# Float64 weights made float32 by a shifted upper word, a sign step and an integer addition, with w_in kept tile by tile

## The chip, the cores and the metric

The kernel runs on one core of one Trainium2 chip. The metric is the device time of one execution in microseconds; before the change its median over three runs is 944.7 us (944.42 to 946.44). The profile was taken on one more execution, whose span, from the first instruction to the last, is 942.4 us.

The core has five engines with queues of their own, which meet through semaphores: TensorE (PE in the profile; its weight loads are PEld), VectorE (DVE), ScalarE (ACT), GpSimd (POOL) and SyncE (SP), which here issues most transfers. Instructions of one engine run in the order of the program.

## What is computed

Two blocks, one after the other: an attention without softmax with an RMS norm, and a two-matrix feed-forward block with the gate h * erf(softplus(h)).

```python
# q, k, v: (8, 8, 576, 64) float32; g_norm: (64,) float32
kv = np.einsum('bhsd,bhse->bhde', k, v)
out = np.einsum('bhsd,bhde->bhse', q, kv)
rms = np.sqrt(np.mean(out * out, axis=-1, keepdims=True) + 1e-06)
attn = (out / rms * g_norm).astype(np.float32)
x = attn.transpose(0, 2, 1, 3).reshape(4608, 512)
# w_in: (512, 2048), w_out: (2048, 512), both float64
h = x @ w_in
sp = np.maximum(h, 0.0) + np.log1p(np.exp(-np.abs(h)))
g = h * erf(sp)
result = (g @ w_out).astype(np.float32)
```

The weights come as float64 (a random float32 array times a float64 scalar). [...] the kernel reads them as pairs of 32-bit words, a lower and an upper one, and makes float32 values of them itself, on VectorE and ScalarE, in its first 125 us.

## The kernel before

The 4608 tokens are worked on in nine groups of 512: eight of one batch each (the last 64 rows of each batch are collected in a ninth group). `FC` is 16, the number of 128-wide tiles of the hidden dimension; `KC` is 4, the number of 128-row blocks of the model dimension. A pass of the first two groups uses float32 matmuls with w_in and w_out as they stand in SBUF; from the second group on the operands are cut into three reduced forms (high, low, both), which the later groups fetch from DRAM.

w_in stands in SBUF with the row block outermost, w_out with the tile outermost:

```python
w_in_sb = first_w.tile([P, KC, DF], FP32, name="w_in_sb")
w_out_sb = first_w.tile([P, FC, DM], FP32, name="w_out_sb")
```

A unit of weights is one tile (`k` = 1, the first four tiles of w_in: 128 partitions x 512 values) or a pair (`k` = 2, all else: 128 x 1024). Each goes through a load, a split and a join. Four raw buffers hold what was loaded:

```python
    w_raw, w_cv = {}, {}
    RAW = 4

    def load_w(which, f, k):
        t = w_raw[which, f] = early.tile([P, 2 * G * k], I32, name="w_raw", tag="w_raw", bufs=RAW)
        if which == "in":
            nc.sync.dma_start(
                out=t.rearrange("p (c f) -> p c f", c=KC),
                in_=moe_w_in.rearrange("(c p) f -> p c f", p=P)[:, :, 2 * f * P : 2 * (f + k) * P],
            )
        else:
            nc.sync.dma_start(
                out=t.rearrange("p (t f) -> p t f", t=k),
                in_=moe_w_out.rearrange("(t p) f -> p t f", p=P)[:, f : f + k, :],
            )

    def w_split(which, f, k):

        hi = w_raw[which, f].rearrange("p (n two) -> p n two", two=2)[:, :, 1]
        e = early.tile([P, G * k], I32, name="w_e", tag="w_e", bufs=2)
        m = early.tile([P, G * k], I32, name="w_m", tag="w_m", bufs=2)
        nc.vector.tensor_scalar(
            out=e,
            in0=hi,
            scalar1=20,
            scalar2=0x7FF,
            op0=ALU.logical_shift_right,
            op1=ALU.bitwise_and,
        )
        nc.scalar.activation(e, e, AF.Relu, scale=float(1 << 23), bias=exp_col)
        nc.vector.tensor_scalar(
            out=m, in0=hi, scalar1=0xFFFFF, scalar2=None, op0=ALU.bitwise_and
        )
        nc.scalar.activation(m.bitcast(FP32), m, AF.Identity, scale=2.0**-20, bias=1.0)
        w_cv[which, f] = e, m

    def w_join(which, f, k):
        raw, (e, m) = w_raw.pop((which, f)), w_cv.pop((which, f))
        hi = raw.rearrange("p (n two) -> p n two", two=2)[:, :, 1]
        lo = raw.bitcast(U32).rearrange("p (n two) -> p n two", two=2)[:, :, 0]
        nc.vector.scalar_tensor_tensor(
            out=e, in0=hi, scalar=-(1 << 31), in1=e, op0=ALU.bitwise_and, op1=ALU.bitwise_or
        )
        m = m.bitcast(FP32)
        nc.vector.scalar_tensor_tensor(
            out=m, in0=lo, scalar=2.0**-52, in1=m, op0=ALU.mult, op1=ALU.add
        )
        e = e.bitcast(FP32)
        if which == "in":
            out_ = w_in_sb[:, :, f * P : (f + k) * P]
            e, m = (t.rearrange("p (c f) -> p c f", c=KC) for t in (e, m))
        else:
            out_ = w_out_sb[:, f : f + k, :]
            e, m = (t.rearrange("p (c f) -> p c f", c=k) for t in (e, m))
        nc.vector.tensor_tensor(out=out_, in0=e, in1=m, op=ALU.mult)
```

The split takes the exponent and the mantissa out of the upper word on VectorE (L207, L216) and turns each into a float on ScalarE (L215, L219). The join puts the sign on the power of two (L226), adds the lower word to the mantissa (L230), and multiplies the two (L240).

The units and when they are due, and where they stand in the opening, before the first hidden tile. `first` holds the attention pieces of the four head pairs of group 0, in the order products, apply, halve, mean, norm:

```python
    w_order = sorted(
        [(f, "in", f, 1) for f in range(4)]
        + [(f, "in", f, 2) for f in range(4, FC, 2)]
        + [(min(f + LAG, (f + FC) // 2 + 1), "out", f, 2) for f in range(0, FC, 2)]
    )
    w_at = {"load": 0, "split": 0, "join": 0}
... # cut
    w_rounds = {
        1: ("split",),
        2: ("join", "load", "split"),
        3: ("join", "load"),
        5: ("split",),
        6: ("split", "join", "load", "join", "load"),
    }
    banks_0 = {"kv_ps": (ps_at, "at"), "qt_ps": (ps_h, "h"), "ms_ps": (ps_h, "h")}
    first = [attention(0, p, banks_0 | {"se_ps": (ps_o, f"o{p}")}) for p in range(NP)]
    for i in range(NP + 3):
        for piece, p in ((0, i), (1, i - 1), (4, i - 3), (3, i - 2)):
            if 0 <= p < NP:
                first[p][piece]()
        if i == 1:
            for _ in range(RAW - 2):
                w_next("load")
            load_pair(NP)
            load_pair(NP + 1)
        for what in w_rounds.get(i, ()):
            w_next(what)
```

The attention pieces that stand between them (`bank` gives a PSUM bank; in the opening `qt_ps` and `ms_ps` share the two banks of `ps_h`):

```python
def apply():
    qT, o_ps, kv_ps = st["qT"], bank("se_ps"), st.pop("kv")
    nc.tensor.matmul(kv_ps[:, o_tail], lhsT=bd, rhs=st.pop("tail"), start=True, stop=True)
    nc.tensor.matmul(o_ps, lhsT=bd, rhs=qT, start=True, stop=True)                     # L325
    nc.vector.tensor_copy(out=x_last[:, p, T * R : T * R + R], in_=kv_ps[:, o_tail])   # L326
    st["o"] = o_ps
    nc.scalar.activation(qT, o_ps, AF.Square)                                          # L328

def mean(table=True):
    ms = st["ms"] = bank("ms_ps")
    ... # cut
    nc.tensor.matmul(ms, lhsT=mean_w.bitcast(FP32), rhs=u, start=True, stop=True)      # L351
    ... # cut
    nc.scalar.activation(r, ms, AF.Ln, bias=eps_col)                                   # L358
    nc.scalar.activation(r, r, AF.Exp, scale=-0.5)                                     # L359
    nc.scalar.activation(u, r, AF.Square)                                              # L360
    if table and (T > 0 or p == NP - 1):
        softplus_table()                                                               # L106

def norm():
    ms, u, r = (st.pop(name) for name in ("ms", "u", "r"))
    nc.vector.scalar_tensor_tensor(
        out=u, in0=ms, scalar=EPS, in1=u, op0=ALU.add, op1=ALU.mult
    )
    nc.vector.scalar_tensor_tensor(
        out=u, in0=u, scalar=3.0, in1=r, op0=ALU.subtract, op1=ALU.mult
    )
    if T < FIRST:
        if T not in xT:
            xT[T] = wide.tile([P, KC, G], FP32, name="xT", tag="ab"[T])
        x = xT[T][:, p, :]
    else:
        x = st["x"] = x_new.tile([P, G], FP32, name="x", tag="x")
    nc.vector.scalar_tensor_tensor(
        out=x,
        in0=st.pop("o"),
        scalar=gm_col,
        in1=u,
        op0=ALU.mult,
        op1=ALU.mult,
    )
```

(The norm's three VectorE instructions have the lines L366, L369 and L378 in the profile; the last writes xT.) The hidden tiles of the first group start with two tiles side by side, block by block of xT:

```python
            if n > 1:
                plain[n] = ps_h.tile([P, G], FP32, name="h_ps", tag="h")
                blocks = [(n, c) for c in range(KC)]
            elif n == 0:
                for i, (pool, tag) in enumerate(((ps_at, "at"), (ps_o, "o0"))):
                    plain[i] = pool.tile([P, G], FP32, name="h_ps", tag=tag)
                blocks = [(i, c) for c in range(KC - 1) for i in range(2)] + [(0, KC - 1)]
            else:
                blocks = [(1, KC - 1)]
            for i, c in blocks:
                nc.tensor.matmul(
                    plain[i],
                    lhsT=w_in_sb[:, c, i % FC * P : i % FC * P + P],
                    rhs=xT[T][:, c, :],
                    start=(c == 0),
                    stop=(c == KC - 1),
                )
            ... # cut
            if n in plain:
                nc.scalar.copy(h, plain.pop(n))                # L705
            ... # cut
            nc.scalar.activation(s, h, AF.Softplus)            # L720
            if n == 0:
                w_next("split")
```

In the second group w_in_sb's tiles that are used up become the place for the forms of six tiles of w_out, which are stored to DRAM from there:

```python
parts = w_in_sb.bitcast(FP32R)[:, :, 3 * place * P : 3 * (place + 1) * P].rearrange(
    "p c (i f) -> p i c f", i=3
)
... # cut
for i in range(3):
    if t is None:
        nc.sync.dma_start(
            out=kept[:, i].rearrange("p (c f) -> p c f", c=KC), in_=parts[:, i].bitcast(FP32)
        )
```

Of the kernel before, what the change touches and what calls it, by code (L numbers as in the profile page):

```python
# [60 lines left out]
def kernel(  # L61
# [101 lines left out]
    w_in_sb = first_w.tile([P, KC, DF], FP32, name="w_in_sb")  # L163
# [11 lines left out]
    exp_col = const.tile([P, 1], FP32, name="exp_col")  # L175
    nc.vector.memset(exp_col, -896.0 * (1 << 23))
# [12 lines left out]
    def load_w(which, f, k):  # L189
        t = w_raw[which, f] = early.tile([P, 2 * G * k], I32, name="w_raw", tag="w_raw", bufs=RAW)  # L190
        if which == "in":
            nc.sync.dma_start(
                out=t.rearrange("p (c f) -> p c f", c=KC),
                in_=moe_w_in.rearrange("(c p) f -> p c f", p=P)[:, :, 2 * f * P : 2 * (f + k) * P],
            )
# [5 lines left out]

    def w_split(which, f, k):

        hi = w_raw[which, f].rearrange("p (n two) -> p n two", two=2)[:, :, 1]
        e = early.tile([P, G * k], I32, name="w_e", tag="w_e", bufs=2)
        m = early.tile([P, G * k], I32, name="w_m", tag="w_m", bufs=2)
        nc.vector.tensor_scalar(  # L207
            out=e,
            in0=hi,
            scalar1=20,  # L210
            scalar2=0x7FF,
            op0=ALU.logical_shift_right,
            op1=ALU.bitwise_and,
        )
        nc.scalar.activation(e, e, AF.Relu, scale=float(1 << 23), bias=exp_col)  # L215
        nc.vector.tensor_scalar(  # L216
            out=m, in0=hi, scalar1=0xFFFFF, scalar2=None, op0=ALU.bitwise_and
        )
        nc.scalar.activation(m.bitcast(FP32), m, AF.Identity, scale=2.0**-20, bias=1.0)  # L219
        w_cv[which, f] = e, m  # L220

    def w_join(which, f, k):
        raw, (e, m) = w_raw.pop((which, f)), w_cv.pop((which, f))
        hi = raw.rearrange("p (n two) -> p n two", two=2)[:, :, 1]
        lo = raw.bitcast(U32).rearrange("p (n two) -> p n two", two=2)[:, :, 0]
# [3 lines left out]
        m = m.bitcast(FP32)  # L229
        nc.vector.scalar_tensor_tensor(  # L230
            out=m, in0=lo, scalar=2.0**-52, in1=m, op0=ALU.mult, op1=ALU.add
        )
# [683 lines left out]
```

## Time and profile before

| stretch (us) | what runs | TensorE busy | VectorE busy | ScalarE busy | DMA share |
|---|---|---|---|---|---|
| 0 to 36 | attention of group 0, first weights, first hidden tiles | 24.66 | 20.34 | 20.38 | 0.84 |
| 36 to 145 | first group, the other weights | 109.00 | 91.11 | 90.07 | 0.49 |
| 145 to 240 | second group, weights cut into forms and stored | 95.00 | 77.69 | 66.81 | 0.89 |
| 240 to 936 | the other seven groups | 695.57 | 551.03 | 438.39 | 0.84 |

The columns are busy microseconds within the stretch, and the mean busy share of the core's 16 DMA engines. The mean clock granted to TensorE is 0.999 of full speed.

How to read the profile's lines: a timeline line has the start (us from the span's beginning), the length of the piece, engine, source line, operation, output and inputs, and shape; in brackets, the idle time before it and what ended it. A line of the groups has the count after x, then the busy time in us and the mean of one in ns, then the idle time of the engine just before these instructions and what ended most of it. A line of the waits says who waited for whom: us in total, how often, the longest. A float32 matmul of 128x512 appears as two MATMUL instructions. Ends of matmuls are modelled, so pieces on PE can overlap by a fraction of a microsecond.

### The profile page before, as it was taken

Reading aid. Unit: us, or ns where it says so; the run is one execution under the profiler, and the core shown is the slowest. Engines: PE = TensorE matmul, PEld = TensorE weight load, DVE = VectorE, ACT = ScalarE, POOL = GpSimd, SP = SyncE. Lnnn points to the kernel's source line nnn. Section 1 sums busy time; section 2 is a strip of 40 time slices with the busy share of each in tenths; the row PEclk is TensorE's granted clock in tenths of the full one; section 3 lists DMA queues with packets and bytes.
Section 4 is the critical chain, followed back from the end, with each engine's and each line's share of the span. In section 5 each row is a group of like instructions: output and inputs, shape, how many; then the busy total and the mean of one; then the engine's idle time right before and its main releaser. Section 6 shows DMA issues by size and latency. Waiting matters only on the chain.

```text
span 942.4 us, 11743 instructions
## 1 busy us (share of the span) xinstructions
PE 924.8 (98%) x4272; PEld 683.4 (73%) x4272; DVE 742.6 (79%) x1056; ACT 615.6 (65%) x825; POOL 2.4 (0%) x10
## 2 busy tenths in 40 slices
PE   6999999999999999999999999999999999999997
PEld 4444445666688888888888888888888888888886
DVE  3999858887577787877778888878887877787667
ACT  3899776776766666666666666666666666665551
POOL 1000000000000000000000000000000000000000
PEclk9999999999999999999999999999999999999999
DMA  9766406899699998998899889998896778778871
GB/s 257 276 204 207 150 1 227 318 351 335 214 363 335 309 325 283 306 311 307 280 287 314 294 298 309 311 303 296 293 325 260 263 253 345 284 286 287 353 263 46
DMA packets 111842, 259.78 MB, mean 276 GB/s; under 512 B 43864, under 2 KB 69544, under 8 KB 111784
## 3 DMA queue, kind: packets, MB, share of 16 engines
q1 hardware_dynamic: 110152, 256.73, 78.7%
q10 hardware_dynamic: 1568, 2.29, 0.8%
q8 instruction: 34, 0.56, 0.2%
q14 instruction: 24, 0.20, 0.1%
q0 software_dynamic: 64, 0.00, 0.0%
HBM read 224.40 MB, written 34.60 MB: 275 GB/s over the span
## 4 chain that ended last, share of the span: by engine, by line
PE 92%; DVE 4%; DMA 2%; ACT 1%; issue 0%; SPq 0%; DVEq 0%
PE n_ps L462 45%; PE m_ps L462 22%; PE o_ps L520 10%; PE h_ps L692 6%; PE se_ps L325 3%; PE kv_ps L297 2%; PE qt_ps L319 2%; DMA w_raw<-in_moe_w_in_dram 1%; PE ms_ps L351 1%; DMA v_sb<-in_v_dram 1%; DVE h L876 1%; DVE e L445 1%; PE ms_ps L346 1%; PE ms_ps L347 1%; PE kv_ps L324 1%; DVE e L440 0%
## 5 line engine op out<-in xcount | busy, mean ns | idle before, releaser
L462 PE MATMUL n_ps<-x_forms,w_in_parts 128*128 128x512 f32 x896 | 232.5, 401 | 0.1
L462 PE MATMUL n_ps<-w_out_parts,g_forms 128*128 128x512 f32 x928 | 231.2, 391 | 0.0
L462 PEld LDWEIGHTS n_ps<-w_out_parts,g_forms 128*128 128x128 f32 x928 | 174.2, 188 | 38.4 <-issue 1.4
L462 PEld LDWEIGHTS n_ps<-x_forms,w_in_parts 128*128 128x128 f32 x896 | 166.8, 188 | 43.1 <-issue 9.3
L852 ACT ACTIVATE s<-h 128x512 f32<-128x512 f32 x112 | 71.0, 633 | 178.9 <-DVE h L445 178.9
L445 DVE TENSOR_TENSOR h<-m_ps,h 128x512 f32<-128x512 f32 x116 | 79.7, 687 | 59.8 <-ACT h L837 43.8
L462 PE MATMUL m_ps<-w_out_parts,g_forms 128*128 128x512 f32 x464 | 124.2, 389 | 0.0
L462 PE MATMUL m_ps<-x_forms,w_in_parts 128*128 128x512 f32 x448 | 120.0, 390 | 0.0
L520 PE MATMUL o_ps<-w_out_sb,h_sb 128*128 128x512 f32 x224 | 100.8, 593 | 0.3 <-DVE h_sb L642 0.3
L462 PEld LDWEIGHTS m_ps<-w_out_parts,g_forms 128*128 128x128 f32 x464 | 87.1, 188 | 18.0
L462 PEld LDWEIGHTS m_ps<-x_forms,w_in_parts 128*128 128x128 f32 x448 | 84.1, 188 | 17.7
L445 DVE TENSOR_TENSOR e<-m_ps,e 128x512 f32<-128x512 f32 x116 | 80.2, 692 | 18.2 <-PE m_ps L462 10.9
L440 DVE SCALAR_TENSOR_TENSOR e<-n_ps,e 128x512 f32<-128x512 f32 x88 | 60.3, 685 | 39.2 <-PE n_ps L462 39.2
L520 PEld LDWEIGHTS o_ps<-w_out_sb,h_sb 128*128 128x128 f32 x224 | 42.3, 190 | 48.9 <-issue 46.6
L411 DVE SCALAR_TENSOR_TENSOR g_forms<-g_forms 128x1024 fp32r<-128x1024 f32 x58 | 71.1, 1225 | 2.0
L408 DVE TENSOR_TENSOR g_forms<-h,g_forms 128x1024 fp32r<-128x1024 f32 x58 | 70.6, 1217 | 1.7 <-ACT g_forms L405 1.4
L876 DVE TENSOR_TENSOR h<-h,s 128x1024 f32<-128x1024 f32 x58 | 68.3, 1218 | 0.7 <-ACT s L856 0.7
L837 ACT ACTIVATE h<-n_ps 128x512 f32<-128x512 f32 x112 | 65.5, 585 | 3.4 <-PE n_ps L462 3.4
L405 ACT ACTIVATE g_forms<-h 128x1024 fp32r<-128x1024 f32 x58 | 58.9, 1059 | 12.2 <-PE m_ps L462 8.7
L692 PE MATMUL h_ps<-xT,w_in_sb 128*128 128x512 f32 x144 | 64.9, 594 | 0.7 <-DVE w_in_sb L240 0.6
L106 ACT ACT_TABLE_LOAD x44 | 56.5, 1283 | 0.8
L856 ACT ACTIVATE s<-s 128x1024 f32<-128x1024 f32 x56 | 56.2, 1052 | 0.3
(98 smaller groups left out, 1013.3 us busy)
## 6 DMA issues: line engine op xcount, KB each, us to landing
w_out_parts<-w_out SPq DMA_DIRECT2D x116, 768.0 KB
w_in_parts<-w_in SPq DMA_DIRECT2D x112, 768.0 KB
w_in<-w_new SPq DMA_DIRECT2D x16, 768.0 KB
q_sb<-in_q_dram SPq DMA_DIRECT2D x32, 256.0 KB
w_raw<-in_moe_w_out_dram SPq DMA_DIRECT2D x8, 1024.0 KB
out_dram<-e SPq DMA_DIRECT2D x32, 256.0 KB
k_sb<-in_k_dram SPq DMA_DIRECT2D x28, 287.5 KB
v_sb<-in_v_dram SPq DMA_DIRECT2D x28, 287.5 KB
```

What stands on the lines that cost most here:

```text
L106: nc.scalar.preload_act_table_set("softplus")
L405: nc.scalar.activation(high, x, AF.Copy, scale=1.0 + 2.0**-13)
L408: nc.vector.tensor_tensor(out=low, in0=x, in1=high.bitcast(FP32), op=ALU.subtract)
L411: nc.vector.scalar_tensor_tensor(out=both, in0=low.bitcast(FP32), scalar=SHIFT, in1=high.bitcast(FP32), op0=ALU.mult, op1=ALU.add,)
L440: nc.vector.scalar_tensor_tensor(out=out_, in0=ps, scalar=scale, in1=out_, op0=ALU.mult, op1=ALU.add)
L445: nc.vector.tensor_tensor(out=out_, in0=ps, in1=out_, op=ALU.add)
L462: nc.tensor.matmul(ps, lhsT=weights(form, k), rhs=moving(form, k), start=(form == forms[0] and k == 0), stop=(form == forms[-1] and k == 3),)
L520: nc.tensor.matmul(o_ps[j], lhsT=g[:, j * P : j * P + P], rhs=w_out_sb[:, f, :], start=(f == 0), stop=last,)
L692: nc.tensor.matmul(plain[i], lhsT=w_in_sb[:, c, i % FC * P : i % FC * P + P], rhs=xT[T][:, c, :], start=(c == 0), stop=(c == KC - 1),)
L837: nc.scalar.activation(h[:, i], n_ps, AF.Copy, scale=SHIFT - 1.0)
L852: nc.scalar.activation(s[:, i], h[:, i], AF.Softplus)
L876: nc.vector.tensor_tensor(out=part(h, half), in0=part(h, half), in1=part(s, half), op=ALU.mult)
```

## The change

The conversion to float32 is done in another way. The upper word of a float64, read as a float32, has the sign, eleven bits of exponent of which three fall into the mantissa's place, and twenty bits of mantissa. ScalarE multiplies this float by 2^-112, which rebases the exponent; VectorE shifts the bits left by three, so exponent and mantissa come to stand where float32 has them, and puts the sign bit back; the top bits of the lower word, scaled by 2^-29 on ScalarE and rounded to an integer, are added as integers. Two steps of VectorE in the split and two of three in the join give way to one shift and one addition; the two ScalarE steps now read the raw words, every second 32-bit word of them, and no longer the output of a VectorE step. A bias column of 4 bytes per partition is no longer needed.

w_in is kept tile by tile, [tile, row block, column], so that a unit's result is one contiguous run; a pair of tiles is loaded by two transfers with rows of 1 KB, where it was one with rows of 2 KB. The weight forms that are put into w_in_sb's place, and stored from there, become contiguous runs too: 2 KB where they were four of 512 bytes.

The diff in full, but for its header:

```diff
@@ -160,7 +160,7 @@
             load_last(0, 0)
             load_last(0, 1)
 
-    w_in_sb = first_w.tile([P, KC, DF], FP32, name="w_in_sb")
+    w_in_sb = first_w.tile([P, FC, KC, P], FP32, name="w_in_sb")
     w_out_sb = first_w.tile([P, FC, DM], FP32, name="w_out_sb")
 
 
@@ -172,8 +172,6 @@
     for i in range(2):
         nc.vector.memset(mean_f[i * D : i * D + D, i * D : i * D + D], 1.0 / D)
     nc.vector.tensor_copy(out=mean_w, in_=mean_f)
-    exp_col = const.tile([P, 1], FP32, name="exp_col")
-    nc.vector.memset(exp_col, -896.0 * (1 << 23))
     eps_col = const.tile([P, 1], FP32, name="eps_col")
     nc.vector.memset(eps_col, EPS)
     bd_kv = const.tile([P, 2, P], FP32, name="bd_kv")
@@ -189,55 +187,54 @@
     def load_w(which, f, k):
         t = w_raw[which, f] = early.tile([P, 2 * G * k], I32, name="w_raw", tag="w_raw", bufs=RAW)
         if which == "in":
-            nc.sync.dma_start(
-                out=t.rearrange("p (c f) -> p c f", c=KC),
-                in_=moe_w_in.rearrange("(c p) f -> p c f", p=P)[:, :, 2 * f * P : 2 * (f + k) * P],
-            )
+            for i in range(k):
+                cols = slice(2 * (f + i) * P, 2 * (f + i + 1) * P)
+                nc.sync.dma_start(
+                    out=t[:, 2 * G * i : 2 * G * (i + 1)].rearrange("p (c f) -> p c f", c=KC),
+                    in_=moe_w_in.rearrange("(c p) f -> p c f", p=P)[:, :, cols],
+                )
         else:
             nc.sync.dma_start(
                 out=t.rearrange("p (t f) -> p t f", t=k),
                 in_=moe_w_out.rearrange("(t p) f -> p t f", p=P)[:, f : f + k, :],
             )
 
+    def words(which, f):
+
+        raw = w_raw[which, f]
+        hi, lo = (
+            raw.bitcast(kind).rearrange("p (n two) -> p n two", two=2)[:, :, half]
+            for kind, half in ((FP32, 1), (U32, 0))
+        )
+        return hi, lo, raw.rearrange("p (n two) -> p n two", two=2)[:, :, 1]
+
     def w_split(which, f, k):
 
-        hi = w_raw[which, f].rearrange("p (n two) -> p n two", two=2)[:, :, 1]
+
+        hi, lo, _ = words(which, f)
         e = early.tile([P, G * k], I32, name="w_e", tag="w_e", bufs=2)
         m = early.tile([P, G * k], I32, name="w_m", tag="w_m", bufs=2)
+        nc.scalar.activation(e.bitcast(FP32), hi, AF.Copy, scale=2.0**-112)
+        nc.scalar.activation(m, lo, AF.Copy, scale=2.0**-29)
+        w_cv[which, f] = e, m
+
+    def w_join(which, f, k):
+
+
+        hi = words(which, f)[2]
+        e, m = w_cv.pop((which, f))
+        w_raw.pop((which, f))
         nc.vector.tensor_scalar(
-            out=e,
-            in0=hi,
-            scalar1=20,
-            scalar2=0x7FF,
-            op0=ALU.logical_shift_right,
-            op1=ALU.bitwise_and,
-        )
-        nc.scalar.activation(e, e, AF.Relu, scale=float(1 << 23), bias=exp_col)
-        nc.vector.tensor_scalar(
-            out=m, in0=hi, scalar1=0xFFFFF, scalar2=None, op0=ALU.bitwise_and
-        )
-        nc.scalar.activation(m.bitcast(FP32), m, AF.Identity, scale=2.0**-20, bias=1.0)
-        w_cv[which, f] = e, m
-
-    def w_join(which, f, k):
-        raw, (e, m) = w_raw.pop((which, f)), w_cv.pop((which, f))
-        hi = raw.rearrange("p (n two) -> p n two", two=2)[:, :, 1]
-        lo = raw.bitcast(U32).rearrange("p (n two) -> p n two", two=2)[:, :, 0]
+            out=e, in0=e, scalar1=3, scalar2=None, op0=ALU.logical_shift_left
+        )
         nc.vector.scalar_tensor_tensor(
             out=e, in0=hi, scalar=-(1 << 31), in1=e, op0=ALU.bitwise_and, op1=ALU.bitwise_or
         )
-        m = m.bitcast(FP32)
-        nc.vector.scalar_tensor_tensor(
-            out=m, in0=lo, scalar=2.0**-52, in1=m, op0=ALU.mult, op1=ALU.add
-        )
-        e = e.bitcast(FP32)
         if which == "in":
-            out_ = w_in_sb[:, :, f * P : (f + k) * P]
-            e, m = (t.rearrange("p (c f) -> p c f", c=KC) for t in (e, m))
+            out_ = w_in_sb[:, f : f + k].rearrange("p t c f -> p (t c f)")
         else:
-            out_ = w_out_sb[:, f : f + k, :]
-            e, m = (t.rearrange("p (c f) -> p c f", c=k) for t in (e, m))
-        nc.vector.tensor_tensor(out=out_, in0=e, in1=m, op=ALU.mult)
+            out_ = w_out_sb[:, f : f + k, :].rearrange("p t f -> p (t f)")
+        nc.vector.tensor_tensor(out=out_.bitcast(I32), in0=e, in1=m, op=ALU.add)
 
 
     w_order = sorted(
@@ -478,11 +475,9 @@
             parts = t.rearrange("p i (c f) -> p i c f", c=KC)
         else:
             t = None
-            parts = w_in_sb.bitcast(FP32R)[:, :, 3 * place * P : 3 * (place + 1) * P].rearrange(
-                "p c (i f) -> p i c f", i=3
-            )
+            parts = w_in_sb.bitcast(FP32R)[:, 3 * place : 3 * (place + 1)]
         if which == "in":
-            x = w_in_sb[:, :, f * P : f * P + P]
+            x = w_in_sb[:, f]
         else:
             x = w_out_sb[:, f, :].rearrange("p (c f) -> p c f", c=KC)
         upper_w(x, parts[:, 0])
@@ -691,7 +686,7 @@
             for i, c in blocks:
                 nc.tensor.matmul(
                     plain[i],
-                    lhsT=w_in_sb[:, c, i % FC * P : i % FC * P + P],
+                    lhsT=w_in_sb[:, i % FC, c],
                     rhs=xT[T][:, c, :],
                     start=(c == 0),
                     stop=(c == KC - 1),
```

More of the change, by code (lines that the diff above doesn't have):

```diff
@@ L200, in load_w @@
             )
+    def words(which, f):
[5 more added lines that the diff above has]
+        return hi, lo, raw.rearrange("p (n two) -> p n two", two=2)[:, :, 1]
     def w_split(which, f, k):
[L204 removed]
+        hi, lo, _ = words(which, f)
         e = early.tile([P, G * k], I32, name="w_e", tag="w_e", bufs=2)
         m = early.tile([P, G * k], I32, name="w_m", tag="w_m", bufs=2)
[L207 to L219 removed]
+        nc.scalar.activation(e.bitcast(FP32), hi, AF.Copy, scale=2.0**-112)
+        nc.scalar.activation(m, lo, AF.Copy, scale=2.0**-29)
         w_cv[which, f] = e, m
     def w_join(which, f, k):
[L223 to L225 removed]
+        hi = words(which, f)[2]
+        e, m = w_cv.pop((which, f))
+        w_raw.pop((which, f))
+        nc.vector.tensor_scalar(
+            out=e, in0=e, scalar1=3, scalar2=None, op0=ALU.logical_shift_left
+        )
         nc.vector.scalar_tensor_tensor(
```

## The prediction, made before the changed kernel was run

> **What bounds the kernel now.** I read the page first, then who waits for whom on TensorE, then the timelines of TensorE and VectorE in the first 45 us. The page's first lines:
>
> ```profile
> span 942.4 us, 11743 instructions
> ...
> PE 924.8 (98%) x4272; PEld 683.4 (73%) x4272; DVE 742.6 (79%) x1056; ACT 615.6 (65%) x825; POOL 2.4 (0%) x10
> ```
>
> TensorE is busy for all but 942.4 - 924.8 = 17.6 us. A change that touches neither the matmuls nor those 17.6 us can't move the end. The view of waits, TensorE alone, whole run (total us, times, longest):
>
> ```profile
> PE kv_ps L297 <- DMA v_sb<-in_v_dram: 8.9, 4, 6.5
> PE ms_ps L351 <- ACT rms_r L358: 1.3, 1, 1.3
> PE h_ps L692 <- DVE w_in_sb L240: 0.6, 1, 0.6
> PE kv_ps L305 <- DMA q_last<-in_q_dram: 0.4, 1, 0.4
> PE o_ps L520 <- DVE h_sb L642: 0.3, 1, 0.3
> ```
>
> That is 11.5 us, 11.2 of it ahead of 36 us; the other 6 us are the tail: the last matmul ends at 936.6, and only the last sums and stores follow. The table of busy time by stretches agrees: between 36 and 240 us TensorE is busy 100% of each stretch, although VectorE stands at 19.3 of 20 us and ScalarE at 19.5 of 20 between 60 and 80. So the weight conversion, which runs from 14 to 125 us, matters in its first 22 us alone. TensorE's timeline there (start, length, idle before):
>
> ```profile
> 27.03 1.10 PE L351 MATMUL ms_ps<-qT,mean_w 128*128 128x512 f32 x2 [1.28 <-ACT rms_r L358]
> 27.96 7.36 PE L692 MATMUL h_ps<-xT,w_in_sb 128*128 128x512 f32 x16
> 35.95 7.13 PE L692 MATMUL h_ps<-xT,w_in_sb 128*128 128x512 f32 x16 [0.62 <-DVE w_in_sb L240]
> ```
>
> and VectorE's, which from 21.95 to 43 us has hardly a gap:
>
> ```profile
> 24.14 0.68 DVE L226 SCALAR_TENSOR_TENSOR w_e<-w_raw,w_e 128x512 int32<-128x512 int32 x1
> 24.74 0.68 DVE L230 SCALAR_TENSOR_TENSOR w_m<-w_raw,w_m 128x512 f32<-128x512 uint32 x1
> 25.46 0.69 DVE L240 TENSOR_TENSOR w_in_sb<-w_e,w_m 128x512 f32<-128x512 f32 x1
> ...
> 26.20 0.68 DVE L366 SCALAR_TENSOR_TENSOR qT<-ms_ps,qT 128x512 f32<-128x512 f32 x1
> ...
> 30.42 0.42 DVE L207 TENSOR_SCALAR w_e<-w_raw 128x512 int32<-128x512 int32 x1
> ...
> 32.53 0.75 DVE L378 SCALAR_TENSOR_TENSOR xT<-se_ps,gm_col,qT 128x512 f32<-128x512 f32 x1
> 33.20 0.42 DVE L207 TENSOR_SCALAR w_e<-w_raw 128x512 int32<-128x512 int32 x1
> ...
> 35.20 0.69 DVE L240 TENSOR_TENSOR w_in_sb<-w_e,w_m 128x512 f32<-128x512 f32 x1
> ```
>
> Three points to see. The mean of the last pair (27.03) is put down to ScalarE's L358; but the bank it wants is read last by VectorE's L366 of the pair two before, which ends at 26.88 and stands behind tile 1's join (24.14 to 26.07). The first 16 hidden matmuls take 7.36 us where 16 at the steady 0.43 us (3.43 us per 8, from the chain) take 6.86: their last blocks need the xT written at 32.53, ready at 33.28. And tile 2, written at 35.20, releases 35.95. So all three losses are VectorE's queue, and weight work stands in front of each.
>
> [...] The groups of the first 160 us, shapes apart, agree (busy us, mean ns):
>
> ```profile
> L226 DVE SCALAR_TENSOR_TENSOR w_e<-w_raw,w_e 128x1024 int32<-128x1024 int32 x14 | 17.2, 1230 | 3.0 <-ACT w_e L215 3.0
> L215 ACT ACTIVATE w_e<-w_e,exp_col 128x1024 int32<-128x1024 int32 x14 | 16.0, 1145 | 7.0 <-DVE w_e L207 7.0
> L219 ACT ACTIVATE w_m<-w_m 128x1024 f32<-128x1024 int32 x14 | 14.6, 1042 | 0.0
> L207 DVE TENSOR_SCALAR w_e<-w_raw 128x1024 int32<-128x1024 int32 x14 | 9.6, 686 | 0.5 <-DMA w_raw<-in_moe_w_out_dram 0.5
> ```
>
> [...] L226 reads such a stride in 1230 ns and L240, contiguous, takes 1225: [...] ScalarE reads no such stride before. [...] at 20 to 21 us, when nearly only the 1 KB rows of single w_in tiles move, 383 GB/s at a DMA share of 1.08; at 39 to 40 us, 2 KB rows of a w_in pair, 401 at 1.03. That is 355 against 389 GB/s per full share, 9% less.
>
> **The change part by part.** All durations are the rows of before.
>
> Removed on VectorE: per pair (128x1024, 14 of them) L207 686 ns, L216 688, L230 1223. Added: a shift, one source, like L207: 686. The sign step is L226 again; the integer addition takes L240's place (int32 and fp32 rows cost the same, 1230 and 1225). So 5.05 us become 3.14: -1.91 per pair. Per single tile (128x512, 4 of them): 418 + 419 + 686 + 686 + 692 = 2.90 become 418 + 686 + 692 = 1.80: -1.10. Sum: 14 x 1.91 + 4 x 1.10 = 31 us less VectorE, 742.6 to about 711. Nearly all of it is hidden: after 36 us TensorE waits for none of it.
>
> ScalarE: two ACTIVATE become two, reading w_raw with a stride: 1145 + 1042 become about 2 x 1050 (a scaled copy, 128x1024 SBUF to SBUF, L405, is 1059). About -1 us in all, hidden. But its split no longer waits for VectorE (7.0 us of idle on L207).
>
> On the path, with starts. A join's three steps now depend on each other: shift 0.42 + 0.03, sign 0.68 + 0.03, addition to the next start 0.61 = 1.77, against 1.93 (24.14 to 26.07).
> - Tile 1's join: 24.14 to 25.91, so the L366 of 26.20 starts at 26.04, the mean at 26.87, the hidden matmuls at 27.80: 0.16 earlier.
> - Then L366, L369, L378 of pair 1 end at 28.15; pair 2 waits for ScalarE's square as now and ends about 30.33. The split of 30.42 to 31.09 is gone, so pair 3 follows at once if its ScalarE chain (now ending 30.1) lets it: three steps of 0.72, 0.72, 0.66 put xT's last block at about 32.5 instead of 33.28. Needed at 27.80 + 12 x 0.43 = 32.96. So the 16 matmuls take 6.86: next issue at 34.66.
> - Tile 2: ScalarE's table load (1.28) after 30.05, split 31.35 to 32.5; VectorE, without the 0.67 of L207 and L216 at 33.20, joins from 32.6 to 34.3. Ready just ahead of 34.66. The hidden matmuls of tile 2 start at about 34.7 instead of 35.95: **1.25 us earlier**.
> - Tile 3 is joined by about 36, needed at 38.1. The pair after it must have landed: at 36.5 or so now, later by 0.3 for its 1 KB packets (1.05 MB at 355 instead of 389 GB/s). Split on ScalarE to 39, join (0.69 + 0.03, 1.22 + 0.03, 1.2 = 3.2) to about 41, needed at 43.1. ScalarE's copy of tile 2's h stands behind the next split (landed 39.8, ends 42.0): 42.6, needed at 43.1. Tight, but it fits.
>
> The six weight tiles that are stored from w_in_sb go out in 2 KB rows instead of 512 B, at 165 to 235 us, where the DMA share is 0.89 to 0.98. Relief, but TensorE waits for no transfer there: 0. From 36 us on, the whole program moves up by the 1.25 us; nothing is added at the tail.
>
> Sum: 944.7 - 1.25 = 943.4.
>
> **The rivals.**
> 1. A new wait takes the gain back: TensorE could stop on the pair of tiles 4 and 5 or on ScalarE's copy behind its split, near 43 us, where I have 0.5 to 2 us of margin. For: the DMA share is 1.0 from 34 to 43 us, and the pair's packets are halved. It would leave 0.3 to 0.8 of the gain: 944.0.
> 2. ScalarE becomes the bound. It is busy 19.5 of 20 us from 60 to 80. If the strided read ran at half rate, each pair would cost 2 us more; 6 pairs to 90 us are 12 us, of which TensorE would lose perhaps half: 950. Against: VectorE's strided rows.
> 3. The vanished 4-byte column moves tiles. In the built program, every tile of the left side allocated after it begins 32 bytes lower, so from a multiple of 256 to an odd multiple of 32: q, k, v, w_raw, x_forms0, half of the weight buffers. For compute engines before shows it is free: x_both lies at such an address, and m_ps<-x_both has 394 ns, n_ps<-x_low, aligned, 395. For transfers into such addresses before shows nothing. [...] If a transfer slowed by 5%, the loads ahead of 20 us would give back up to 1 us: 944.5; at 15% or more the later weight loads (DMA share 0.84 after 260 us) could start to bind.
> 4. Nothing at all: the waits are redistributed, 944.7.
>
> **Range and chances.** My path gives 943.4. Rivals 1, 3 and 4 pull to 944 to 945; the three runs of before spread over 2 us. So 942.0 to 945.2. A gain of 2% would need 18.9 us, more than all the idle time of TensorE: 0.01. A loss of 2% needs rival 2 or a large rival 3: 0.01.
>
> **What would show it.** Right: VectorE at about 711 us busy, 37 instructions or so fewer; the shift near 686 ns; the two new ACTIVATE near 1050; the wait of h_ps on w_in_sb gone or under 0.1; the second block of hidden matmuls at about 34.7; TensorE without a gap from there to the tail. Wrong: a wait of h_ps near 43 us (rival 1); ACTIVATE of 1.5 us or more (rival 2); v_sb landing later than 19.96, or transfers named among TensorE's waits after 260 us (rival 3).

## The result: 1% slower, and where the time went

| | median (us) | runs | ratio to before, 95% interval |
|---|---|---|---|
| before | 944.56 | 944.11 to 946.44 | |
| after | 953.87 | 952.61 to 954.29 | 1.0095 [1.008, 1.0109] |

The changed kernel is slower by 9.3 us, about 1%. The prediction said 943.4 us, within 942.0 to 945.2; it was wrong by 10.5 us.

The page of the changed kernel, its first lines (busy us, share of the span, instructions):

```profile
span 950.8 us, 11753 instructions
...
PE 931.1 (98%) x4272; PEld 683.8 (72%) x4272; DVE 716.8 (75%) x1019; ACT 617.4 (65%) x825; POOL 2.4 (0%) x10
```

VectorE did get its relief, 742.6 to 716.8 us. But TensorE, with the same 4272 matmul instructions, is busy 6.3 us longer (931.1 against 924.8). No wait explains that: matmuls took longer, some at half clock, most without it. The rest is waits; the view of waits for TensorE, whole run (total us, times, longest):

```profile
PE kv_ps L294 <- DMA v_sb<-in_v_dram: 9.6, 2, 7.4
PE h_ps L687 <- ACT h_sb L700: 1.9, 1, 1.9
...
PE kv_ps L294 <- DVE w_in_sb L237: 0.7, 1, 0.7
```

The wait that the change was to remove (h_ps on w_in_sb, 0.6) is gone from its place. In its stead the wait for v in the first 20 us is longer (9.6 against 8.9), another 0.7 of the same products is put down to VectorE, and there is a new one, of 1.9 us, on ScalarE's copy of h. TensorE's timeline shows where it is:

```profile
29.57 13.90 PE L687 MATMUL h_ps<-xT,w_in_sb 128*128 128x512 f32 x32
44.29 0.60 PE L316 MATMUL qt_ps<-ident,q_sb 128*128 128x128 f32 x4
46.82 5.40 PE L687 MATMUL h_ps<-xT,w_in_sb 128*128 128x512 f32 x8 [1.93 <-ACT h_sb L700]
```

The first 32 hidden matmuls run in one piece, 13.90 us: what was two pieces (27.96 and 35.95) with a wait between them. That is the predicted gain, only all of it starts 1.6 us too late (29.57 against 27.96). Then TensorE waits 1.93 us, and the eight matmuls after the wait take 5.40 us; eight take 3.60 elsewhere. The table of stretches tells why (one line of it: stretch, its length, busy us of PE, PEld, DVE, ACT and POOL with counts, then the granted clock, DMA share and GB/s):

```profile
48.00:50.00 2.00, 2.00 (x4) 0.95 (x3) 1.23 (x1) 1.98 (x3) 0.00 (x0) 0.50 1.07 347
```

The clock is 0.50 here, and these matmuls start 0.85 us apart, where the median in this kernel is 0.43; the stretch at half clock lasts 3.41 us (47.61 to 51.03), and costs half of that, 1.7 us. And ScalarE's timeline shows what the copy of h stood behind:

```profile
40.92 1.13 ACT L217 ACTIVATE w_e<-w_raw 128x1024 f32<-128x1024 f32 x1 [3.90 <-DMA w_raw<-in_moe_w_in_dram]
...
44.15 1.14 ACT L217 ACTIVATE w_e<-w_raw 128x1024 f32<-128x1024 f32 x1
45.19 1.11 ACT L218 ACTIVATE w_m<-w_raw 128x1024 int32<-128x1024 uint32 x1
46.20 0.57 ACT L700 COPY h_sb<-h_ps 128x512 f32<-128x512 f32 x1
```

ScalarE sat idle 3.90 us for the weights of tiles 4 and 5, which landed at 40.9, not at the 36.5 of the prediction. The next split and the copy come after it in program order, so the copy starts at 46.20; the prediction had it done at 42.6.

The two kernels issue their matmuls in the same order, so the start of each can be set against its twin. After is 0.9 us behind at the first matmul (as profiled; the first load), 1.6 at 20 us, 0.5 at 36 (the gain was real, and was spent), 2.4 at 44.5 and 4.1 from 52 to 148 us. The pieces that carry the last figure begin at 143.65 (before) and here:

```profile
147.71 2.74 PE L687 MATMUL h_ps<-xT,w_in_sb 128*128 128x512 f32 x6
```

From there the gap first shrinks, to 3.8 at 240 us, and then grows from group to group, to 8.9 us at the last matmul: 4.8 us more, with no new wait of 0.3 us or more in the view. Groups by shape tell in which matmuls. One group of TensorE in the window 350 to 425 us (count, busy us, mean ns), first before, then after:

```profile
L462 PE MATMUL m_ps<-x_forms,w_in_parts 128*128 128x512 f32 x48 | 12.9, 390 | 0.0
```

```profile
L459 PE MATMUL m_ps<-x_forms,w_in_parts 128*128 128x512 f32 x48 | 13.1, 395 | 0.0
```

In the window 260 to 330, one group of tokens earlier, they show 389 and 390. The lengths are modelled; the starts are not, and they say the same more clearly. From start to start the median is 227 ns in each of the seven later groups before. After it is 234 in the second, fourth and sixth of the seven later groups of tokens (their hidden matmuls) and in the last batch of w_out's, and 227 elsewhere. The means of those (leaving out gaps of 260 ns and more) are 5.0 to 6.6 ns higher, over 192 matmuls in each of the three groups and 48 in the last batch: 0.93 + 0.91 + 1.18 + 0.31 = 3.3 of the 4.8 us. Of the rest, gaps of TensorE in the later groups make 0.7 us (the longest from start to start is 0.46); w_out's other batches, with the median unchanged, make 1.1, for a reason that isn't known; and the second group of tokens gives 0.5 back.

What sets the slow groups apart is where their operands lie. As built, the tiles that are allocated on the left side of SBUF after the dropped bias column moved down by 32 bytes, those of the matmuls and transfers named here from a multiple of 256 to 224 modulo 256; the right side didn't move: the later groups' tiles on it are at 0, those of the first two groups (w_in_sb, w_out_sb, x_both) at 224. Of the seven later groups the second, fourth and sixth have their x_forms on the right, and all have their w_in_parts on the left; the other four have both on the left.

### The profile page after: what moved, and what is told of

It is laid out like the page before. It is cut to its first block, busy times and chain, and to the rows that moved or that the text cites. A ratio compares the mean times of both kernels' runs of the same rounds, so it can differ in the third digit from the quotient of the medians.

```text
span 950.8 us, 11753 instructions
## 1 busy us (share of the span) xinstructions
PE 931.1 (98%) x4272; PEld 683.8 (72%) x4272; DVE 716.8 (75%) x1019; ACT 617.4 (65%) x825; POOL 2.4 (0%) x10
## 4 chain that ended last, share of the span: by engine, by line
PE 91%; DVE 3%; ACT 3%; DMA 2%; issue 0%; SPq 0%; DVEq 0%; ACTq 0%
PE n_ps L459 44%; PE m_ps L459 22%; PE o_ps L515 9%; PE h_ps L687 5%; PE se_ps L322 3%; PE kv_ps L294 2%; PE qt_ps L316 2%; PE ms_ps L348 1%; DMA q_last<-in_q_dram 1%; DMA q_sb<-in_q_dram 1%; DVE h L871 1%; DMA w_raw<-in_moe_w_in_dram 1%; DVE e L442 1%; PE ms_ps L344 1%; PE ms_ps L343 1%; PE kv_ps L321 1%
## 5 line engine op out<-in xcount | busy, mean ns | idle before, releaser
L442 DVE TENSOR_TENSOR e<-m_ps,e 128x512 f32<-128x512 f32 x116 | 80.3, 692 | 18.6 <-PE m_ps L459 11.8
L408 DVE SCALAR_TENSOR_TENSOR g_forms<-g_forms 128x1024 fp32r<-128x1024 f32 x58 | 71.1, 1226 | 2.0
L402 ACT ACTIVATE g_forms<-h 128x1024 fp32r<-128x1024 f32 x58 | 58.9, 1059 | 12.6 <-PE m_ps L459 9.9
```

The lines of the kernel that those rows point to most:

```text
L402: nc.scalar.activation(high, x, AF.Copy, scale=1.0 + 2.0**-13)
L408: nc.vector.scalar_tensor_tensor(out=both, in0=low.bitcast(FP32), scalar=SHIFT, in1=high.bitcast(FP32), op0=ALU.mult, op1=ALU.add,)
L442: nc.vector.tensor_tensor(out=out_, in0=ps, in1=out_, op=ALU.add)
```

## The experiments

Two theories stood at the start. **A, the addresses:** the conversion does what was predicted, and the dropped column alone costs all of the loss, by slower transfers into the shifted tiles in the opening and slower matmuls later. **B, the conversion:** its halved packets and the splits in front of ScalarE's copy make the stall at 45 us, and the addresses are free. Medians are in us; each ratio is to before, with its 95% interval.

### 1. The changed kernel with its address put back

```diff
+    const.tile([P, 1], FP32, name="pad_col")
     eps_col = const.tile([P, 1], FP32, name="eps_col")
```

> The changed kernel with an unused 4-byte column in the place of the one that was dropped, so that every tile of the left side is back at its address of before (a multiple of 64 bytes). Theory A, the 32-byte shift of the left side is the cause (slower transfers into SBUF in the opening, then slower matmuls): the loss goes, and the gain of the shorter VectorE queue comes out: about 943.5 us, no wait of h_ps on ScalarE near 45 us, no half-speed stretch of the clock. Theory B, the new split on ScalarE and the halved rows of the w_in pairs are the cause: the stall of about 1.9 us and the half-speed stretch stay, 948 us or more. If both matter: between.

Measured: **943.81** (943.05 to 944.23, 12 runs), 0.9991 [0.9983, 1.0]. Ten us of 954 hang on one unused column of 4 bytes per partition. Its waits of TensorE:

```profile
PE kv_ps L295 <- DMA v_sb<-in_v_dram: 9.1, 4, 6.8
...
PE h_ps L688 <- ACT h_sb L701: 0.4, 1, 0.4
```

and its TensorE timeline:

```profile
27.73 13.90 PE L688 MATMUL h_ps<-xT,w_in_sb 128*128 128x512 f32 x32
...
43.46 3.70 PE L688 MATMUL h_ps<-xT,w_in_sb 128*128 128x512 f32 x8 [0.41 <-ACT h_sb L701]
```

The 32 hidden matmuls run without a gap from 27.73; tile 2 is 1.35 us earlier than before, the last matmul 0.98. The spacing is 227 ns everywhere. The wait on the copy of h is still there, with 0.4 us instead of 1.9. A holds, and the prediction's path with it.

### 2. The kernel before with the address shifted

```diff
-    exp_col = const.tile([P, 1], FP32, name="exp_col")
-    ...
-    eps_col = const.tile([P, 1], FP32, name="eps_col")
+    both_col = const.tile([P, 2], FP32, name="both_col")
+    eps_col, exp_col = both_col[:, 0:1], both_col[:, 1:2]
```

> The kernel before with its two 4-byte columns (epsilon and exponent bias) in one 8-byte tile, so that the left side moves down by the 32 bytes and nothing else changes. Theory A: slower by the 4.7 us that the matmuls lose after 150 us and by 1 to 1.6 us of the opening, about 950.5 us, without a stall at 45 us. Theory B: no change, 944.6 us.

Measured: **954.1** (953.19 to 955.82), 1.0104 [1.0086, 1.0122]: more than A said. The address alone costs as much as the whole change lost, with the old conversion. The surprise is the stall: A had put it down to the new conversion meeting the late weights, but it needs only the late weights.

```profile
PE h_ps L692 <- ACT h_sb L705: 1.5, 1, 1.5
PE se_ps L325 <- ACT qT L320: 1.3, 1, 1.3
```

It is 1.8 us behind at 20 us, 3.3 at 44.5 and 9.3 at the last matmul; m_ps<-x_forms is 395 ns here too. The second of the two waits stands at 235 us and in no other run; it is 1.3 of the 3.6 us by which this kernel exceeds A's 950.5. B falls.

### 3. The shift in the opening alone

```diff
             early_room.close()
+            ctx.enter_context(tc.tile_pool(name="pad", bufs=1)).tile([P, 1], FP32, name="pad")
             late = ctx.enter_context(tc.tile_pool(name="late", bufs=1))
```

The changed kernel, with the left side back on a multiple of 256 from the second group of tokens on.

> The changed kernel with the 32 bytes put back only behind the opening: ahead of the pool of x_forms0 and of all weight buffers that follow; q, k, v and the raw weights of the opening stay at the shifted addresses. Theory A with two separate parts: the opening loses as in the changed kernel (4 us behind the kernel before at 150 us), the drift of 4.7 us after it is gone: about 949.2 us. If transfers alone were at fault in the opening and matmuls not at all, 949 too, but with unchanged matmul spacing. Theory B: 953.9 us.

Measured: **949.56** (948.46 to 950.71), 1.0055 [1.0035, 1.0074]. The spacing is 227 ns again, and the opening keeps its loss: a stall of 1.7 us and 3.41 us at half clock after it. So of the 10.1 us between the changed kernel and its padded twin, 4.3 go with the later tiles' address (953.87 - 949.56) and 5.8 stay (949.56 - 943.81). Not all of the 5.8 is lost in the opening: at 52 us this kernel is 4.1 us behind the padded one (3.15 behind before, which the padded one leads by 0.98). Another 2.3 come later, nearly all between 500 and 700 us and mostly in gaps of TensorE, of which the view puts 0.4 down to transfers into w_in_parts. There all operands agree; why these gaps come isn't known. The forecast of 949.2, 4 us in the opening and no drift, was met partly by luck.

### 4. How far must the address move? By 64, by 128, and both sides

```diff
+    const.tile([P, 24], FP32, name="pad_col")     # 64 modulo 256
+    const.tile([P, 40], FP32, name="pad_col")     # 128 modulo 256
```

One of the two lines each, in the changed kernel; the right side stays at 0.

> The changed kernel with an unused column of 96 bytes in the place of the dropped one: the left side stands 64 bytes above its place before, so at multiples of 64 bytes, but no longer of 128 or 256. If 64 bytes is what counts, for transfers and for matmuls: 943.8 us as with the 4-byte column, v_sb waits of 9 us, matmul spacing unchanged. If 128 or 256 bytes count: the drift of x_forms1 against w_in_parts comes back (2 to 5 us), and the opening is late again (1 to 5 us): 946 to 954 us.

> The changed kernel with an unused column of 160 bytes: the left side stands 128 bytes above its place before, at odd multiples of 128 bytes. With +64 bytes the opening was late and the spacing of x_forms1 against w_in_parts was 3% longer. If 128 bytes is what both need: 943.8 us. If both need 256: about 950 us. If the transfers need 256 and the matmuls 128: late opening, no drift, 945 to 947 us; the other way round: 946 us with a drift of 2 to 4 us.

Measured: 64: **950.07** (949.62 to 951.36), 1.0061 [1.0048, 1.0075]; 128: **949.35** (948.7 to 950.71), 1.0052 [1.0038, 1.0065]. Neither is enough for either effect. The spacing in the groups concerned is 233 and 232 ns, and both stall on the copy of h, 2.1 and 2.0 us; only the second has the stretch at half clock after it (mean granted clock 0.81 from 44 to 48 us and 0.76 from 48 to 52; the first has 1.00 in both).

```diff
-    ... name="shift", bufs=1, side="right")).tile([P, 504], FP32, name="shift")
+    ... name="shift", bufs=1, side="right")).tile([P, 496], FP32, name="shift")   # first
+    ... name="shift", bufs=1, side="right")).tile([P, 512], FP32, name="shift")   # second
```

These move the right side instead: the first to 32 modulo 256, the second to 224, where the left side of the changed kernel is.

> The changed kernel with the right side moved as well (its unused shift tile 32 bytes smaller), so that x_forms1, g_forms and w_out_parts stand at odd multiples of 32 bytes like the left side. If matmuls are slow where their stationary and moving operands stand differently against 64 bytes, the drift of 4.7 us is gone: about 949.2 us. If they are slow for any operand off a multiple of 64 bytes, the drift grows, to 956 us or more, since then all products of the later groups have such operands. Theory B: 953.9 us.

> The changed kernel with the unused tile of the right side 32 bytes larger, so that both sides stand at 224 modulo 256: no operand is at a multiple of 256, and all later operands agree modulo 256. If matmuls slow down only where their two operands differ modulo 256, x_forms1 against w_in_parts is back at the spacing of 227 ns, its MATMUL rows at the mean of before, and what is left of the drift is waits for transfers, which now all land off 256: 949 to 951 us. If any operand off 256 is slow, every later group has 232 to 234 ns: about 960 us.

The first, **951.18** (949.71 to 952.45), 1.0071 [1.0052, 1.009], decides nothing: it was laid out on the guess that only a residue modulo 64 counts, and leaves the operands 64 apart modulo 256. Its spacing is 229 and 233 ns in the groups concerned, between the two answers, and it waits 2.7 us in the later groups where before doesn't (1.3 on transfers into w_in_parts, 1.4 on ScalarE).

The second has a median of **951.96** (945.94, 951.12, 952.8 and 955.04), 1.0086 [1.0064, 1.0108]. Its profiled execution, with a span of 944.1 us, is clear as to the matmuls: all seven later groups are at 227 ns, and the group of 350 to 425 us stands as before:

```profile
L459 PE MATMUL m_ps<-x_forms,w_in_parts 128*128 128x512 f32 x48 | 12.9, 390 | 0.0
```

It is 2.2 us behind at 44.5 us and still only 1.9 at the end: the drift is gone though no operand lies on a multiple of 256. So in these runs the spacing is 227 ns where the two operands *agree* modulo 256, on a multiple of 256 or off it. The runs together give more: with the stationary operand 64 bytes above the moving one, modulo 256, the spacing is 233 ns (experiment 4's 64 bytes, x_forms1; its first right-side kernel, the last batch of w_out), and with it 64 below only 229 (the same two kernels, the other way round). Why the last kernel's other runs took 5 to 9 us more isn't known; none of them was traced.

### 5. Whose transfers are late in the opening?

```diff
+    early.tile([P, 1], FP32, name="pad_raw", bufs=1)
     mean_f = early.tile([P, P], FP32, name="mean_f", bufs=1)
...
+            ctx.enter_context(tc.tile_pool(name="pad", bufs=1)).tile([P, 1], FP32, name="pad")
             late = ctx.enter_context(tc.tile_pool(name="late", bufs=1))
```

Here w_raw is on a multiple of 256 again, and only q, k, v and the attention's own tiles are shifted.

> The changed kernel with 32 bytes put back ahead of the raw weights of the opening and again behind the opening: only q, k, v and the attention's own tiles stay at shifted addresses. With the pad behind the opening alone it was 949.6 us. If the shifted raw weights cause the stall near 45 us by landing late, that stall and the half-speed stretch go, and q, k, v leave 1 to 1.5 us: about 945.5 us. If q, k and v cause it, by filling the queue ahead of the weights: 949 us.

Measured: **947.06** (945.28 to 949.85, 18 runs), 1.0027 [1.0019, 1.0034], between the two answers. The pair of tiles 4 and 5 is still late; ScalarE's first split of it, in this kernel and then in the padded one of experiment 1:

```profile
39.66 1.14 ACT L218 ACTIVATE w_e<-w_raw 128x1024 f32<-128x1024 f32 x1 [3.15 <-DMA w_raw<-in_moe_w_in_dram]
```

```profile
36.98 1.14 ACT L218 ACTIVATE w_e<-w_raw 128x1024 f32<-128x1024 f32 x1 [1.79 <-DMA w_raw<-in_moe_w_in_dram]
```

So the greater part of the delay (2.7 of the changed kernel's 3.9 us against 36.98) comes from q, k and v. The other 1.3 can't be given to the weights' own shift: the changed kernel and the three of experiments 3 and 4 that have its opening show 40.92, 39.99, 39.91 and 40.71. How q, k and v delay the weights stands in SyncE's timeline. The pair's two loads, and the issue of a k ahead of them, in the changed kernel and then in the padded one:

```profile
18.40 3.18 SPq L136 DMA_DIRECT2D k_sb<-in_k_dram  x1
...
34.75 0.94 SPq L192 DMA_DIRECT2D w_raw<-in_moe_w_in_dram  x2
```

```profile
17.15 2.34 SPq L136 DMA_DIRECT2D k_sb<-in_k_dram  x1
...
31.09 0.94 SPq L193 DMA_DIRECT2D w_raw<-in_moe_w_in_dram  x2
```

From the loads' issue to ScalarE's split it is 6.2 us in the one and 5.9 in the other (and 5.9 in this experiment's kernel, issued at 33.75). The pair isn't slow on its way; it is sent 3.7 us later. SyncE's issues stand in the same order in both; in the changed kernel it is 1.25 us behind at this k, and loses the other 2.4 in the issues of q, k and v that follow it, which take longer. The stretch of 5 to 10 us, where they load, in the changed kernel and in the padded one:

```profile
5.00:10.00 5.00, 2.62 (x29) 2.32 (x29) 0.49 (x3) 0.00 (x0) 0.21 (x1) 1.00 1.12 221
```

```profile
5.00:10.00 5.00, 2.85 (x29) 2.32 (x29) 0.74 (x3) 0.32 (x1) 0.21 (x1) 1.00 1.09 267
```

The last two columns: per full DMA share, 221 / 1.12 = 197 GB/s against 267 / 1.09 = 245 (before: 257). With w_raw alone put back it is 189; in all kernels with q, k and v off a multiple of 256 it is 189 to 213, in all with them on it 245 to 262. The engines are as busy, and move about a fifth less. The single packets of the first 20 us tell whose: the mean time of one of 256 bytes (q) is 18.6 to 20.1 ns on a multiple of 256 and 22.4 to 23.5 off it, of one of 1536 bytes (k, v) 82.5 to 89.0 and 92.4 to 103.5, but of one of 1 KB (weights) 56.3 to 61.8 and 57.7 to 61.8. The sources were the same; the place written to, in SBUF, was what differed. Why a packet into such a place takes longer was not shown.

### 6. Can the last 0.4 us be had?

In the padded kernel TensorE still waits 0.4 us on the copy of h behind a split (rival 1). Two ways round it. The first puts that split after the softplus of tile 2, so that the copy doesn't stand behind it:

```diff
         while due(0):
-            weights()
+            if n == 2:
+                w_next("join")
+                w_next("load")
+            else:
+                weights()
...
-            if n == 0:
+            if n in (0, 2):
                 w_next("split")
```

run with the address put back, and without (the changed kernel with only this):

> The changed kernel with the 4-byte column, and the split of the first pair of w_out moved behind ScalarE's copy and softplus of hidden tile 2. The wait of 0.4 us that stands at 43 us (h_ps on ScalarE's h_sb) is put down to ScalarE standing in order behind a split whose words have not landed. If so it goes: 943.4 us, 0.4 below the kernel with the column alone, and TensorE has no gap from 28 us on. If the wait is for the weights of tiles 4 and 5 themselves, it stays or moves to VectorE: 943.8 us.

> The changed kernel, addresses as they are, with the same split moved behind tile 2's copy and softplus. If the stall of 1.9 us near 45 us comes from ScalarE's order, TensorE waits only for the join of tiles 4 and 5 (ready near 45.4 us where TensorE is free at 44.9), the gap is under 1 us, and the half-speed stretch of 3.4 us does not follow: 953.9 - 1.4 - 1.7 = 950.8 us. If the stall is the late transfer whatever the order, 953.9 us.

Measured: with it, **942.9** (942.0 to 946.23, 21 runs), 0.9985 [0.9978, 0.9991]: faster than both kernels. Against the kernel with the column alone (0.9991 [0.9983, 1.0]) the intervals overlap, so that the size of this last step is not shown. The wait is gone, and one of 0.6 on ScalarE's qT turns up at 55.5 us, so the trace doesn't keep the gain whole. Without: **951.3** (950.08 to 951.69), 1.0071 [1.0055, 1.0086], 2.6 below the changed kernel:

```profile
PE n_ps L459 <- DMA w_in_parts<-w_in: 0.7, 1, 0.7
PE h_ps L691 <- DVE w_in_sb L237: 0.7, 1, 0.7
```

The stall at 45 us has shrunk to 0.7, now on the late weights themselves, and the half clock is gone (1.00 from 44 to 52 us); the drift stays, and a later weight transfer is waited for. So 2.6 us of the loss hung on the order of ScalarE's instructions behind one late transfer.

The second way keeps the 2 KB rows of a pair, loaded by one transfer, and lets ScalarE put the words into tile order as it reads them:

```diff
-            for i in range(k):
-                ... # one transfer for each tile, 1 KB rows
+            nc.sync.dma_start(out=t.rearrange("p (c f) -> p c f", c=KC), in_=... )   # 2 KB rows
...
+                t = t.rearrange("p (c t f two) -> p t c f two", c=KC, t=k, two=2)
+                return t[:, :, :, :, i]
```

(for a pair of w_in, the sign step becomes two instructions of 512 values). Then both ways at once:

> The changed kernel with the 4-byte column, and the pairs of w_in loaded by one transfer with rows of 2 KB as before; ScalarE reorders the words on the way, and the sign step of these pairs is two instructions of 512. If the halved rows delay the pair of tiles 4 and 5, ScalarE's wait for it (1.8 us near 37 us) shrinks by some 0.3 us and TensorE's 0.4 us wait by as much: 943.5 us. If rows of 1 KB cost nothing that reaches TensorE: 943.8 us.

> The changed kernel with the 4-byte column, w_in pairs loaded by one transfer with rows of 2 KB, and the split of the first w_out pair behind tile 2's copy and softplus. Each of the last two alone gave 942.9 and 943.0 us. If both remove the same 0.4 us wait at 43 us: 942.9 us. If they add: 942.4 us. TensorE has no gap between 28 us and the tail.

Measured: 2 KB rows, **943.03** (942.22 to 943.94, 20 runs), 0.9985 [0.9979, 0.9992]; both, **943.24** (942.73 to 945.43, 21 runs), 0.9986 [0.998, 0.9993]. The rows also remove the 0.4 (ScalarE's wait for the pair is 1.49 instead of 1.79). The two don't add up: both take away the same wait, and in the kernel with both TensorE has no other wait above 0.3 us between 28 us and the tail.

## Why the prediction was wrong, point by point

- **The conversion's cost: right.** In the changed kernel's first 160 us, by shape (count, busy us, mean ns, then idle time before):

```profile
L217 ACT ACTIVATE w_e<-w_raw 128x1024 f32<-128x1024 f32 x14 | 16.1, 1152 | 4.0 <-DMA w_raw<-in_moe_w_in_dram 3.9
L237 DVE CUSTOM_DVE_ANT_0 w_out_sb<-w_e,w_m 128x2048 uint16<-128x2048 uint16 x8 | 9.8, 1226 | 1.1
L227 DVE TENSOR_SCALAR w_e<-w_e 128x1024 int32<-128x1024 int32 x14 | 9.7, 690 | 13.8 <-ACT w_e L217 13.7
```

  The shift is 690 (said: 686) and the integer addition, which is recorded as a custom instruction on 16-bit halves, 1226 (1225). There are 37 instructions fewer. The durations of all of VectorE's instructions sum to 31 us less (782.5 to 751.8), as worked out; its busy time fell by only 26, since busy time counts overlaps once and the old conversion's independent steps overlapped. The 711 mixed the two measures; nothing hung on it.
- **The strided ACTIVATE: 10% too low.** 1152 ns for every second 32-bit word of w_raw, where 1050 was taken from a contiguous copy (1059). It is no half rate; rival 2 fell.
- **The path, -1.25 us: right, and hidden.** Experiment 1 has tile 2 at 1.35 us and the last matmul at 0.98 us earlier than before, and 943.81 us against the 943.4 of the sum. That the pair would land at 36.5 + 0.3 was right there too (36.98).
- **Rival 1: right in kind.** A wait of h_ps on ScalarE's copy near 43 us, 0.4 us with the address put back. In the changed kernel it is 1.9 us at 45, but there rival 3 made it so large.
- **The step that failed is rival 3, by its size.** It named the shift of 32 bytes and gave it up to 1 us. Measured, it is 10.1 us (experiment 1 against the changed kernel). Two terms were wrong.
  - *"For compute engines before shows it is free."* It compared m_ps<-x_both, 394, with n_ps<-x_low, 395. n_ps can't serve as the yardstick, since its means differ from those of m_ps for other reasons too (n_ps<-x_forms has 406 where m_ps<-x_forms has 390). The clean comparison was m_ps<-x_forms, 390, in the same profile. x_both lay at 224 modulo 256 against w_new at 0, so before already paid for the mismatch there. The window 145 to 240 us shows it, before and then after (where both are at 224):

```profile
L462 PE MATMUL m_ps<-x_both,w_new 128*128 128x512 f32 x52 | 14.2, 395 | 0.0
```

```profile
L459 PE MATMUL m_ps<-x_both,w_new 128*128 128x512 f32 x48 | 12.9, 390 | 0.0
```

  Five nanoseconds of 390 look like nothing; over the 624 matmuls of the slow groups they are 3.3 of the 4.8 us. (The matmuls with w_new together take 0.5 us less in the changed kernel.)
  - *"If a transfer slowed by 5%, the loads ahead of 20 us would give back up to 1 us."* The transfers of 5 to 10 us moved about 20% less per full share (245 to 197 GB/s), and the term stopped at the loads ahead of 20 us. It left out what stands behind them: SyncE sends the next weights 3.7 us late, they land 3.9 us late, ScalarE waits for them in program order, TensorE waits 1.93 us for ScalarE's copy, and its clock drops, for 1.7 us more. The prediction had given its margin there (0.5 to 2 us) and did not ask which rival could eat it.

**Open:** why the matmuls' spacing is longer where their operands differ modulo 256; how the cost depends on the difference (32 and 128 apart cost about the same, 232 to 234 ns, 64 apart less in one direction, 229); what delays the later groups in experiments 3 and 4; what decides whether the clock drops after a stall; and what made three runs of the last address variant slow.

## What to carry to other kernels

Before a change is judged by what it computes, compare the addresses of every tile before and after: a constant that is dropped moves the tiles behind it, and here 4 bytes per partition cost 10.1 us where the rest of the change gained 0.8. Where a comparison in the profile is to show that something is free, compare rows that differ in that alone, and multiply the difference by the count before calling it nothing. And where a margin is small, add up all the rivals that eat it at once: here the pair of weights that landed 3.9 us late held up ScalarE's instructions behind it, and became a wait of 1.93 us on TensorE.

## What the runs showed of the hardware

- A matmul with a 512-column moving operand, in the reduced forms, starts every 227 ns when both operands have the same address modulo 256 (both at 0, 64, 128 or 224), and every 232 to 234 when they are 32, 64 or 128 apart; 229 where the stationary one stands 64 below the moving one (medians of the groups, with addresses as built; before, after, experiments 1 to 4).
- Transfers into SBUF tiles of q, k and v off a multiple of 256 moved 189 to 213 GB/s per full DMA share from 5 to 10 us, against 245 to 262 on it. Packets of 256 bytes took 22.4 to 23.5 ns against 18.6 to 20.1, those of 1536 bytes 92.4 to 103.5 against 82.5 to 89.0; those of 1 KB took about the same, 57.7 to 61.8 against 56.3 to 61.8 (experiment 5).
- The granted clock fell to 0.50 for 3.41 us after a TensorE stall of 1.93 us in the changed kernel, and likewise after stalls of 1.7 us (experiment 3, where the eight matmuls behind the stall take 5.40 us) and 2.0 us (experiment 4, 128 bytes, with 0.81 and 0.76 in the two stretches around it). It didn't fall after stalls of 1.5 us (experiment 2 and experiment 4's first right-side kernel), 1.6 (experiment 5), 1.8 (experiment 4's second right-side kernel) and 2.1 (experiment 4, 64 bytes); in experiments 2 and 5 and that second kernel the eight matmuls behind the stall take 3.67 to 3.70 us. So in these runs the length of the stall alone doesn't decide; what does was not shown.
